# Four row blocks of a weight and two pairs of another transposed by DMA at the turn of a forward-and-backward decode kernel

## The chip, the cores and the metric

The kernel runs on one core of one Trainium2 chip. The time of a run is in device microseconds (us), for the whole kernel in one launch: a forward pass of a small transformer block for one token, and all its gradients. "PE" is the matrix engine (its weight loads are listed as PEld), "DVE" the vector engine, "ACT" the scalar engine, "SP" the engine whose queue issues nearly all DMAs of this kernel, and "POOL" the general-purpose engine. Sixteen DMA engines carry the transfers.

## The reference: what is computed

A block with one query token (x is 1 x 640), 32 heads of 192, and a key and a value cache of 8192 positions for each head. Modulation vectors (shift, scale and gate, twice) come from a second vector c. The attention half adds a gated `attention(h) @ wo`; the second half is a token mixer and an MLP of width 1536. The mixer shifts its channels by one or two tokens, so with one token it adds zeros, and x1 below is the half's input:

```python
def _A_ref(x, k_cache, v_cache, wq, wo):
    q = heads(x @ wq)                                  # 32 heads of 192
    scores = einsum('bhqd,bhkd->bhqk', q, k) * Dh ** (-0.5)
    o = einsum('bhqk,bhkd->bhqd', softmax(scores), v)
    return merged(o) @ wo                              # wo is 6144 x 640
...
h2 = _gelu(_layernorm(x1, axis=-1) @ w3) @ w4          # w3 is 640 x 1536, w4 1536 x 640
...
mod = (_silu(c) @ w_mod).reshape(c.shape[0], 6, 1, -1)
h = _layernorm(x, axis=-1) * (1 + ca) + sa
x = x + ga * _A_ref(h, A_k_cache, A_v_cache, A_wq, A_wo)
h = _layernorm(x, axis=-1) * (1 + cb) + sb
x = x + gb * _B_ref(h, B_w1, B_w2, B_w3, B_w4)
```

The outputs are x and the gradients of x, of both caches, of wq, wo, w3, w4, c and w_mod for a given gradient of x. The gradients of the caches are the largest part: as many bytes are stored as the two caches have.

## The kernel before, in words

**Forward pass.** Heads go by in a software pipeline (loop at line 652). For each head, K and V come in halves or whole (12288 bytes a partition for a half: 32 of the 64 rows that a partition holds, each of 192). DVE multiplies K by the broadcast query, PE sums the products, and the softmax weights scale K and are multiplied with V on PE. K lies in six halves of one large buffer, `k_mem`; V in four halves of `v_mem`. The two heads of a pair share one tile of Wo (`wo_t`, lines 495 to 500), with which `fwd_ao` (line 571) forms that pair's part of `o @ wo`.

**The turn.** When the last head's weights are known, the kernel must, in this order: finish o of heads 30 and 31; form the last two pairs' part of `o @ wo`; do both layer norms; form u = n2 @ W3 (60 products of a 128 x 128 block with one column, `u_mm`); the derivative of gelu and du, which also needs d_g, twelve DVE products of W4's rows with a broadcast vector (`dg_some`, line 594); dn2 = du @ W3 transposed (60 products, line 1050); the way back through the norms to dao, the gradient of the attention's output (`lnb_dao`); and do = dao @ Wo transposed for the last pair (line 1423). Only then can the gradient of V be formed and stored for the last head (line 1427 on).

**Transposed weights before.** dn2 and do take the weights transposed. PE makes them: it multiplies blocks of 128 x 128 with the identity into PSUM, four at a time (`w3T_pe`, line 759; `woT_some`, line 780), and ACT copies each group into SBUF (`w3T_act`). W3 has 60 such blocks, the last pair's Wo 15. These groups are spread by hand between the steps of the turn, through four fill points (`FILL`, lines 794 to 809) and calls in between. For the last pair but one, nothing is transposed: in the first step of the backward pass, DVE multiplies its three Wo blocks with the broadcast dao and sums along the rows (`bwd_ttr`, line 1098, called in `hook(0)`). The other pairs' do are done in batches of up to three pairs (`load_wo`, line 894; `bwd_wo_mult`).

**Loads at the turn.** `load_w` (line 637) puts W4 and W3 into freed halves of `k_mem`. All these DMAs, and the two V halves of head 29 (line 900) and the first batch of Wo (line 1021), stand on SP's queue in program order; a DMA whose buffer is still read waits there, and those behind it wait too. Each DMA also waits for the one eight places before it.

**Backward pass.** Heads go from 31 down (line 1455). For each one V is multiplied by do, summed on PE, and the gradients of V and K are formed by DVE and ACT as outer products and stored, with the other gradients' stores as jobs in between.

**Order.** Instructions of PE, DVE and ACT are pinned to the order of the program text (`pin_order`, line 53); waits between engines come from the tiles that they share. A tile counts as a whole there: the PSUM tile `sm_ps` of head 31 holds the sum of weights, o and the product with Wo side by side, and `kb_ps` holds the sums of the scaled K in its first 384 columns and, behind them (`aux_ps`), the small results of the turn.

Of the kernel before, what the change touches and what calls it, by code (L numbers as in the profile page):

```python
# [20 lines left out]
def kernel(  # L21
# [26 lines left out]
    nc = tc.nc  # L48
# [81 lines left out]
    def mul(out, a, b):  # L130
        nc.vector.tensor_tensor(out=out, in0=a, in1=b, op=ALU.mult)  # L131
# [383 lines left out]
    def fwd_tot(h, sm):  # L515
        nc.tensor.matmul(sm[:, 400:402], lhsT=ones_mat_f, rhs=rowsum[:, h - 1 : h + 1], start=True, stop=True)
# [38 lines left out]
    def fwd_o_last(h, st):  # L555
        _, _, bp, ca_, cb_ = head_split(h)
        c0 = 3 * (h // 2)
        sl = slice(bp, bp + 64)
        for o in (o_col_bf, o_col_f):
            mul(o[:, ca_ : ca_ + 1], st["o_ps"][:, 0:1], rinv_bc[:, h : h + 1])  # L560
            mul(o[sl, cb_ : cb_ + 1], st["o_ps"][sl, 1:2], rinv_bc[sl, h : h + 1])
# [171 lines left out]
    dg_some(2)  # L733
    fwd_keepB(hl - 1, st[hl - 1])
    fwd_tot(hl, sl_["sm"])
    fwd_o_mm(hl, 0, sl_)
    xp = ccol(NDC, "xp")
# [17 lines left out]
    w3T_next = [0, 0]  # L755
    w3T_ps = {}
    NG3 = NFC * NDC // 4

    def w3T_pe(n):
        for g in range(w3T_next[0], min(w3T_next[0] + n, NG3)):  # L760
            b = g % 6
            if b in (2, 4):
                w3T_ps[g] = bank("s", 2, "t_ps", SB[0])
                w3T_ps[g + 1] = w3T_ps[g][:, 512:1024]
            elif b < 2:
                w3T_ps[g] = bank("ab"[b], name="t_ps")
            for k in range(4):
                i, f = divmod(4 * g + k, NFC)
                nc.tensor.matmul(w3T_ps[g][:, k * P : (k + 1) * P], lhsT=w3n(i, f * P, (f + 1) * P), rhs=ident_bf, start=True, stop=True)
        w3T_next[0] += n  # L770

    def w3T_act(n):
        for g in range(w3T_next[1], min(w3T_next[1] + n, NG3)):
            if g % 6 in (3, 5) and g > 3:
                continue
            m = 2 if g % 6 in (2, 4) and g > 3 and g + 1 < NG3 else 1
            nc.scalar.copy(out=w3T(4 * g // NFC, 4 * g % NFC, 4 * m), in_=w3T_ps[g][:, 0 : 512 * m])
        w3T_next[1] += n

    def woT_some(n):  # L780
        for g in range(woT_next[0], min(woT_next[0] + n, 4)):
            t_ps = bank("s", 2, "t_ps", SB[0])
            blks = range(4 * g, min(4 * g + 4, 3 * NDC))
            for k, blk in enumerate(blks):
                nc.tensor.matmul(t_ps[:, k * P : (k + 1) * P], lhsT=woT[:, blk * P : (blk + 1) * P], rhs=ident_bf, start=True, stop=True)
            nc.scalar.copy(out=woT[:, 512 * g : 512 * g + P * len(blks)], in_=t_ps[:, 0 : P * len(blks)])
        woT_next[0] += n

    woT = st[HQ - 1]["wo"].rearrange("p c r -> p (c r)")
    woT_next = [0]  # L790
    fwd_ao(HH - 1, sl_["wo"], sl_["sm"], 408, False)
    ao_ps = sl_["sm"][:, 408 : 408 + NDC]
    w3T_pe(1)
    def fill0():
        w3T_act(1)
        w3T_pe(1)

    def fill1():
        w3T_act(1)
        fwd_kvK(hl - 1, 3, st[hl - 1])  # L800

    def fill2():
        pass

    def fill3():
        bwd_pf_act(HS[0])
        w3T_act(4)

    FILL = [fill0, fill1, fill2, fill3]
# [12 lines left out]
    m_ps = aux_ps[:, 64:65]  # L822

    def mean_mm(x):
        nc.tensor.matmul(m_ps, lhsT=ones_mat_f, rhs=x, start=False, stop=True, skip_group_check=True)

    mean_mm(sxp)
# [4 lines left out]
    FILL[0]()  # L832
# [3 lines left out]
    FILL[1]()  # L836
# [8 lines left out]
    w3T_t = tw.tile([P, JH, DH], BF16, name="w3T_t", tag="w3T_t").rearrange("p j d -> p (j d)")  # L845
# [3 lines left out]
    wo_src = {(PS[k], cc): st[2 * PS[k] + 1]["wo"][:, cc, :] for k in range(2) for cc in range(3)}  # L849
# [50 lines left out]
    V_b[HS[2]] = {0: load_v(bv, HS[2], 0, 4), 1: load_v(bv, HS[2], 1, 5)}  # L900
# [22 lines left out]
    w3T_pe(4)  # L923
# [5 lines left out]
    FILL[2]()  # L929
# [7 lines left out]
    FILL[3]()  # L937
# [63 lines left out]
    for i in range(NDC):  # L1001
        u_mm(i)
        if i == 2:
            w3T_pe(1)
            w3T_act(1)
        elif i == 3:
            woT_some(2)
# [3 lines left out]
    dg_some(3)  # L1011
    lnb_sums()
    w3T_pe(3)
# [5 lines left out]
    w3T_pe(5)  # L1019
    w3T_act(8)  # L1020
    load_wo(0, big_tile("V_sb"))
    lnb_map1()
    dg_some(1)
# [10 lines left out]
    def du_cols(lo, hi):  # L1034
        stt(du_bf[:, lo:hi], deriv[:, lo:hi], -1.0, d_g[:, lo:hi], ALU.mult, ALU.mult)

    f_late = dg_next[0]
    du_cols(0, f_late)
    dg_some(NFC)
    du_cols(f_late, NFC)  # L1040
# [5 lines left out]
    for i in range(NDC):  # L1046
        if i == NDC - 1:
            woT_some(1)
        for f in range(NFC):
            nc.tensor.matmul(dn2_ps[:, i : i + 1], lhsT=w3T(i, f), rhs=du_bf[:, f : f + 1], start=False, stop=(f == NFC - 1), skip_group_check=True)  # L1050
    mid_ps = {"h2": aux_ps[:, 32 : 32 + NDC]}
# [7 lines left out]
    nc.scalar.copy(out=kb_sb, in_=kb_ps[:, 0 : 2 * DH])  # L1059
# [38 lines left out]
    def bwd_ttr(hp, cc):  # L1098
        nc.vector.tensor_tensor_reduce(out=wo_src[hp, cc], in0=wo_src[hp, cc], in1=dao_bc, scale=1.0, scalar=0.0, op0=ALU.mult, op1=ALU.add, accum_out=dof[:, 3 * hp + cc : 3 * hp + cc + 1])

# [12 lines left out]

    def fin_do(lo, n):
        sl = slice(3 * lo, 3 * (lo + n))
        dve_copy(do_bf[:, sl], dof[:, sl])
# [273 lines left out]
    wo_first = [(PS[1], cc) for cc in range(3)]  # L1390
# [27 lines left out]

    do_ps = aux_ps[:, 24:27]
    for cc in range(3):  # L1420
        for j in range(NDC):
            blk = cc * NDC + j
            nc.tensor.matmul(do_ps[:, cc : cc + 1], lhsT=woT[:, blk * P : (blk + 1) * P], rhs=dao_bf[:, j : j + 1], start=False, stop=(j == NDC - 1), skip_group_check=True)
    dve_copy(do_bf[:, 3 * PS[0] : 3 * PS[0] + 3], do_ps[:, 0:3])
# [132 lines left out]
```

## Time and profile before

| | |
|---|---|
| median of 3 runs (lowest, highest) | 1362.57 us (1361.49, 1363.54) |
| the profiled execution: time, span | 1363.16 us, 1361.2 us |
| mean granted clock of PE | 0.788 |
| busy PE, PEld, DVE, ACT | 867.7, 622.0, 1083.7, 914.3 us |
| moved by DMA | 567.62 MB, mean 417 GB/s |
| HBM read, written | 339.94 MB, 225.91 MB |
| the chain of waits, by engine | DMA 41%, PE 18%, DVE 16%, ACT 5% |

The span is the time from the first to the last instruction of the profiled execution; its own time is a little longer. No engine is busy for the whole span, and the parts of the pass differ: from 20 to 500 us PE is busy for 443.41 of 480 us, from 700 to 1340 us DVE for 507.15 of 640 us. A line of the groups gives the line of the source, the engine, the operation with output and input tiles, how often it ran, the busy time, the mean length of one in ns, and the idle time ahead of it. Lines of the chain of waits give start, length and work. A window's line gives each engine's busy time, and then the granted clock, the busy share of the DMA engines and the GB/s.

### The profile page before, as it was taken

To read this page: it belongs to the slowest core of one execution; us is meant where nothing else is said; L and a number is where in the kernel's file an instruction comes from. 1 tells how busy PE (TensorE), PEld (TensorE's weight loads), DVE (VectorE), ACT (ScalarE), POOL (GpSimd) and SP (SyncE) were. 2 spreads that over 40 slices of the span, in tenths; PEclk is the share of its full clock that TensorE was granted. 3 is DMA by queue.
4 is the path that set the end of the run, shared out by engine and by line. 5 is a ranking of instruction groups with operands and counts; after the bars stand their busy time and mean duration, and the time that the engine had idled before them with its cause. 6 is when DMAs were issued, how large, how long until landed. Compare 5 with 4: busy or idle time off the path is not lost.

```text
span 1361.2 us, 27663 instructions
## 1 busy us (share of the span) xinstructions
PE 867.7 (64%) x11403; PEld 622.0 (46%) x11406; DVE 1083.7 (80%) x1247; ACT 914.3 (67%) x2558; POOL 3.2 (0%) x10
## 2 busy tenths in 40 slices
PE   4698999999999999847666754443333543242422
PEld 3577777777777777736555642111121111010100
DVE  3488888888888887899988977877668978786875
ACT  0387788778788885876767966765467745666570
POOL 0000000000000000000000000000000000000000
PEclk9799999999999999576776676676666776676766
DMA  9999999999999999799999999999999999999997
GB/s 391 417 422 428 424 416 428 425 409 427 424 417 419 422 423 401 280 396 393 426 422 427 427 431 431 430 431 430 425 433 429 432 427 428 423 434 430 433 431 335
DMA packets 46282, 567.62 MB, mean 417 GB/s; under 512 B 4685, under 2 KB 6989, under 8 KB 19405
## 3 DMA queue, kind: packets, MB, share of 16 engines
q1 hardware_dynamic: 46126, 565.86, 98.7%
q8 instruction: 89, 1.46, 0.4%
q14 instruction: 37, 0.30, 0.1%
q10 hardware_dynamic: 30, 0.00, 0.0%
HBM read 339.94 MB, written 225.91 MB: 416 GB/s over the span
## 4 chain that ended last, share of the span: by engine, by line
DMA 41%; PE 18%; DVE 16%; ACT 5%; issue 3%; DVEq 0%; SPq 0%; ACTq 0%
DMA out_dram<-k_mem 18%; DMA v_mem<-in_A_v_cache_dram 16%; DVE k_mem L1211 7%; PE dP_ps L1230 5%; PE ps_a L471 5%; ACT k_mem L1235 4%; DVE v_mem L131 3%; DMA k_mem<-in_A_k_cache_dram 3%; DMA V_sb<-in_w_mod_dram 3%; PE ps_b L482 2%; DMA out_dram<-dwo 2%; PE S_ps L411 1%; PE kb_ps L488 1%; DVE prod L131 1%; DVE V_sb L131 1%
## 5 line engine op out<-in xcount | busy, mean ns | idle before, releaser
L1235 ACT ACTIVATE k_mem<-do_pb,PF 128x192 bf16<-128x192 bf16 x1086 | 378.9, 441 | 123.7 <-DMA out_dram<-k_mem 87.7
L1230 PE MATMUL dP_ps<-v_mem,ident_bf 128*128 128x512 bf16 (+2 forms) x960 | 219.7, 403 | 264.8 <-DVE v_mem L131 264.8
L446 ACT ACTIVATE EK<-k_mem,E_f 128x192 bf16<-128x192 bf16 x992 | 355.0, 444 | 36.8 <-issue 19.4
L1230 PEld LDWEIGHTS <-ident_bf 128*128 128x128 bf16 x1056 | 120.1, 119 | 381.0 <-DVE v_mem L131 211.9
L1211 DVE TENSOR_TENSOR k_mem<-dS,q_pb 128x6144 bf16<-128x6144 bf16 x62 | 205.5, 3354 | 50.6 <-DMA out_dram<-k_mem 50.3
L131 DVE TENSOR_TENSOR v_mem<-v_mem,do_pb 128x6144 bf16<-128x6144 bf16 (+1 forms) x62 | 199.1, 3249 | 32.7 <-DMA v_mem<-in_A_v_cache_dram 32.7
L131 DVE TENSOR_TENSOR prod<-k_mem,q_pb 128x6144 bf16<-128x6144 bf16 x62 | 207.6, 3349 | 4.5 <-DMA k_mem<-in_A_k_cache_dram 3.2
L471 PE MATMUL ps_a<-EK,v_mem 128*128 128x193 bf16 x1984 | 191.5, 248 | 16.0 <-DMA v_mem<-in_A_v_cache_dram 14.8
L471 PEld LDWEIGHTS <-v_mem 128*128 128x128 bf16 x1984 | 163.7, 98 | 34.4 <-DMA v_mem<-in_A_v_cache_dram 19.7
L453 DVE TENSOR_TENSOR EK<-k_mem,P2h 128x1536 bf16<-128x1536 bf16 x124 | 117.8, 950 | 0.0
L482 PE MATMUL ps_b<-EK,v_mem 128*64 128x193 bf16 x1984 | 106.6, 249 | 0.0
L411 PE MATMUL S_ps<-prod,ident_bf 64*64 64x256 bf16 x2976 | 94.5, 273 | 6.9 <-DVE prod L131 6.9
L411 PEld LDWEIGHTS <-ident_bf 64*64 64x64 bf16 x3072 | 83.9, 109 | 26.3 <-issue 24.1
L482 PEld LDWEIGHTS <-v_mem 128*64 128x64 bf16 x1984 | 79.7, 109 | 19.1 <-issue 15.5
L1211 DVE TENSOR_TENSOR k_mem<-P2h,do_pb 128x2304 bf16<-128x2304 bf16 (+2 forms) x56 | 74.3, 1359 | 11.0 <-DMA out_dram<-k_mem 10.2
L188 ACT CAST do_pb<-bc_ps 128x384 bf16<-128x384 f32 x15 | 7.1, 472 | 96.6 <-PE bc_ps L184 96.6
L488 PE MATMUL kb_ps<-EK,hot_bf 128*32 128x384 bf16 x992 | 63.5, 333 | 0.0
L451 DVE CAST EK<-E_f 128x16 bf16<-128x16 f32 x124 | 24.4, 197 | 32.5 <-ACT EK L446 22.6
L432 ACT ACTIVATE E_f<-sm_ps,negm 128x64 f32<-128x64 f32 x31 | 9.7, 314 | 58.8 <-DVE negm L430 58.8
L415 DVE TENSOR_REDUCE S<-S_ps 128x128 f32<-128x1024 f32 x32 | 39.2, 1225 | 11.1 <-PE S_ps L411 11.0
L1339 PEld LDWEIGHTS <-ident_bf 128*128 128x128 bf16 x100 | 11.7, 117 | 75.4 <-issue 69.6
L1235 ACT ACTIVATE xt<-do_pb,PF 128x192 bf16<-128x192 bf16 x120 | 41.8, 440 | 0.1
(341 smaller groups left out, 843.2 us busy)
## 6 DMA issues: line engine op xcount, KB each, us to landing
v_mem<-in_A_v_cache_dram SPq DMA_DIRECT2D x47, 3072.0 KB, 19.5
out_dram<-k_mem SPq DMA_DIRECT2D x41, 3072.0 KB, 27.0
k_mem<-in_A_k_cache_dram SPq DMA_DIRECT2D x20, 3072.0 KB, 14.6
out_dram<-k_mem SPq DMA_DIRECT2D x33, 1536.0 KB, 19.9
v_mem<-in_A_v_cache_dram SPq DMA_DIRECT2D x25, 1536.0 KB, 16.6
k_mem<-in_A_k_cache_dram SPq DMA_DIRECT2D x24, 1536.0 KB, 18.7
out_dram<-xt SPq DMA_DIRECT2D x3, 3072.0 KB
wq<-in_A_wq_dram SPq DMA_DIRECT2D x3, 2560.0 KB, 31.2
```

The source lines that it names most:

```text
L131: nc.vector.tensor_tensor(out=out, in0=a, in1=b, op=ALU.mult)
L411: nc.tensor.matmul(st["S_ps"][c0 : c0 + 64, r, t * JH : (t + 1) * JH, :], lhsT=ident_bf[64 * r : 64 * r + 64, 64 * r : 64 * r + 64], rhs=p ...
L415: nc.vector.reduce_sum(out=st["S2"], in_=st["S_ps"], axis=AX.X)
L446: nc.scalar.activation(out=st["EK"][q][:, jj, 0:DH], in_=K_st[h, t][:, r * JQ + jj, :], func=ACT.Copy, scale=st["E_f"][:, j : j + 1])
L451: nc.vector.tensor_copy(out=EK[:, :, DH : DH + 1], in_=st["E_f"][:, q * JQ : (q + 1) * JQ, None])
L453: nc.vector.tensor_tensor(out=EK[:, NA:JQ, 0:DH].rearrange("p j (d r) -> p j d r", r=2), in0=K_st[h, t][:, r * JQ + NA : (r + 1) * JQ, :]. ...
L471: nc.tensor.matmul(st["A_ps"][:, 0:n], lhsT=V_sb[:, r * JQ + jj, a0:a1], rhs=EK[:, jj, 0:n], start=(q == 0 and jj == 0), stop=(q == 3 and ...
L482: nc.tensor.matmul(st["B_ps"][g : g + 64, 0:n], lhsT=V_sb[:, r * JQ + jj, b0:b1], rhs=EK[:, jj, 0:n], start=(q == 0 and jj < 2), stop=(q = ...
L488: nc.tensor.matmul(kb_ps[g : g + 32, 0 : 2 * DH], lhsT=hot_bf[:, HQ - 1 - h : 2 * HQ - 1 - h], rhs=EK[:, jj : jj + 2, 0:DH], start=(h == 0 ...
L1211: nc.vector.tensor_tensor(out=o.rearrange("p j (d r) -> p j d r", r=2), in0=pairs[:, :, None, :].to_broadcast([P, n, NP2, 2]), in1=vec.rea ...
L1230: nc.tensor.matmul(bst[h]["dP_ps"][:, t * JH + r : t * JH + r + n, :], lhsT=ident_bf, rhs=V_sb[:, :, k * w : (k + 1) * w], start=(k == 0), ...
L1235: nc.scalar.activation(out=o[:, jj, :], in_=vec_of(do_pb, h), func=ACT.Copy, scale=bst[h]["PF"][:, t * JH + jj : t * JH + jj + 1])
```

## The change

W4's remaining five row blocks are now loaded ahead of W3. Of W3, only row block 0 is still transposed on PE, in three groups. Row blocks 1 to 4 are read a second time from HBM by four transposing DMAs, into the buffer that before took the second half of head 29's V; that half is now loaded after the dn2 products. The Wo tiles of the last two pairs are overwritten by two transposing DMAs, and both pairs' do are formed on PE; the three DVE products and the copy in `hook(0)` are gone. The Wo product of the last pair but one moves in front of the o products of the last head, and both late Wo products are gathered in `aux_ps`. The mean of the first part of x1 is formed between the two halves of o. `fwd_o_last` writes the bf16 column first, then the Wo product follows, then the fp32 column. Three d_g products change place. The copy of `kb_sb` moves from behind dn2 to the norms.

```diff
-        elif k == 1:
-            for i in range(2):
-                nc.sync.dma_start(out=w_t[1][:, i * F : (i + 1) * F], in_=B_w3[i * P : (i + 1) * P, :])
-        else:
+        elif k == 2:
             nc.sync.dma_start(out=w_t[2][:, 0 : 5 * D]..., in_=B_w4[7 * P : 12 * P, :]...)
-            for i in range(2, 4):
+            for i in range(4):
                 nc.sync.dma_start(out=w_t[1][:, i * F : (i + 1) * F], in_=B_w3[i * P : (i + 1) * P, :])
...
-    fwd_keepB(hl - 1, st[hl - 1])
     fwd_tot(hl, sl_["sm"])
+    ao_ps = aux_ps[:, 65 : 65 + NDC]
+    fwd_ao(HH - 2, st[hl - 2]["wo"], aux_ps, 65, False)
+    fwd_rinv(hl, sl_["sm"])
+    fwd_keepB(hl - 1, st[hl - 1])
     fwd_o_mm(hl, 0, sl_)
+    fwd_o_prev(hl - 1)
...
-    fwd_rinv(hl, sl_["sm"])
-    fwd_o_prev(hl - 1)
+    mean_mm(sxp)
     dg_some(3)
     fwd_o_mm(hl, 1, sl_)
-    fwd_o_last(hl, sl_)
-    fwd_ao(HH - 2, st[hl - 2]["wo"], sl_["sm"], 408, False)
+    fwd_o_last(hl, sl_, o_col_bf)
+    fwd_ao(HH - 1, sl_["wo"], aux_ps, 65, False)
+    fwd_o_last(hl, sl_, o_col_f)
...
+    def w3T_pe(g):
+        ps = bank("ab"[g % 2], name="t_ps")
+        for k in range(4):
+            f = 4 * g + k
+            nc.tensor.matmul(ps[:, k * P : (k + 1) * P], lhsT=w3n(0, f * P, (f + 1) * P), rhs=ident_bf, start=True, stop=True)
+        nc.scalar.copy(out=w3T(0, 4 * g, 4), in_=ps)
+
+    woT = {k: st[2 * (HH - 1 - k) + 1]["wo"].rearrange("p c r -> p (c r)") for k in range(2)}
...
-    FILL[0]()
+    dg_some(1)
+    w3T_pe(0)
...
-    FILL[1]()
+    dg_some(1)
+    fwd_kvK(hl - 1, 3, st[hl - 1])
+    w3T_pe(1)
...
-    V_b[HS[2]] = {0: load_v(bv, HS[2], 0, 4), 1: load_v(bv, HS[2], 1, 5)}
+    w3T_t = flat(v_tile(bv, 5))
+    for i in range(1, NDC):
+        nc.sync.dma_start(out=w3T(i, 0, NFC).rearrange("p (f r) -> p f r", r=P), in_=B_w3[i * P : (i + 1) * P, :], transpose=True)
+    for k in range(2):
+        nc.sync.dma_start(out=woT[k].rearrange("p (j r) -> p j r", r=3 * P), in_=A_wo[3 * PS[k] * P : 3 * (PS[k] + 1) * P, :], transpose=True)
+    V_b[HS[2]] = {0: load_v(bv, HS[2], 0, 4)}
...
-    w3T_pe(4)
...
-    FILL[2]()
+    nc.scalar.copy(out=kb_sb, in_=kb_ps[:, 0 : 2 * DH])
...
-    FILL[3]()
+    w3T_pe(2)
+    bwd_pf_act(HS[0])
...
-        woT_some(1)
...
         u_mm(i)
-        if i == 2:
-            w3T_pe(1)
-            w3T_act(1)
-        elif i == 3:
-            woT_some(2)
...
-    dg_some(3)
     lnb_sums()
-    w3T_pe(3)
+    dg_some(NFC)
...
-    w3T_pe(5)
-    w3T_act(8)
     load_wo(0, big_tile("V_sb"))
-    lnb_map1()
-    dg_some(1)
...
-    f_late = dg_next[0]
-    du_cols(0, f_late)
-    dg_some(NFC)
-    du_cols(f_late, NFC)
+    stt(du_bf, deriv, -1.0, d_g, ALU.mult, ALU.mult)
+    lnb_map1()
     lnb_map2()
...
+    V_b[HS[2]][1] = load_v(bv, HS[2], 1, 5)
...
-    nc.scalar.copy(out=kb_sb, in_=kb_ps[:, 0 : 2 * DH])
...
         if i == 0:
-            for u in wo_first:
-                bwd_ttr(*u)
-            fin_do(PS[1], 1)
             bwd_dob(PS[1])
...
+    do_mm(0)
+    do_out(0)
     do_pb[PS[0]] = pair_bc2(bsm, do_bf, PS[0], "do_pb")
-    o0 = tw.tile([P, JH, DH], BF16, name="dV", tag="w3T_t")
+    o0 = tw.tile([P, JH, DH], BF16, name="dV")
     bwd_dv_dve(o0, HS[0], 0, 0, (8, 16, JH))
+    do_mm(1)
     h2_mm()
+    do_out(1)
```

`do_mm(k)` is the loop of 15 products of line 1423 for one of the two pairs, with the blocks in the order in which the transposing DMA lays them; `do_out(k)` is the copy behind it.

More of the change, by code (lines that the diff above doesn't have):

```diff
@@ L553, in fwd_o_prev, with fwd_o_last @@
         dve_copy(o_col_bf[bp : bp + 64, cb_ : cb_ + 1], o_col_f[bp : bp + 64, cb_ : cb_ + 1])
-    def fwd_o_last(h, st):
+    def fwd_o_last(h, st, o):
         _, _, bp, ca_, cb_ = head_split(h)
@@ L558, in fwd_o_last @@
         sl = slice(bp, bp + 64)
-        for o in (o_col_bf, o_col_f):
-            mul(o[:, ca_ : ca_ + 1], st["o_ps"][:, 0:1], rinv_bc[:, h : h + 1])
-            mul(o[sl, cb_ : cb_ + 1], st["o_ps"][sl, 1:2], rinv_bc[sl, h : h + 1])
+        mul(o[:, ca_ : ca_ + 1], st["o_ps"][:, 0:1], rinv_bc[:, h : h + 1])
+        mul(o[sl, cb_ : cb_ + 1], st["o_ps"][sl, 1:2], rinv_bc[sl, h : h + 1])
     def fwd_o_rows(hp, sm):
@@ L740, with mean_mm @@
     nc.vector.tensor_tensor_reduce(out=T5[:, 0, :], in0=xp, in1=ZW[:, 0, :], scale=-1.0 / D, scalar=0.0, op0=ALU.mult, op1=ALU.add, accum_out=sxp)
-    fwd_rinv(hl, sl_["sm"])
-    fwd_o_prev(hl - 1)
+    m_ps = aux_ps[:, 64:65]
+    def mean_mm(x):
+        nc.tensor.matmul(m_ps, lhsT=ones_mat_f, rhs=x, start=False, stop=True, skip_group_check=True)
+    mean_mm(sxp)
     dg_some(3)
     fwd_o_mm(hl, 1, sl_)
-    fwd_o_last(hl, sl_)
-    fwd_ao(HH - 2, st[hl - 2]["wo"], sl_["sm"], 408, False)
+    fwd_o_last(hl, sl_, o_col_bf)
+    fwd_ao(HH - 1, sl_["wo"], aux_ps, 65, False)
+    fwd_o_last(hl, sl_, o_col_f)
     SB = [1024]
@@ L753, in w3T @@
         return w_t[2][:, 5 * D + f * P : 5 * D + (f + n) * P]
[L755 to L787, printed above, removed]
@@ L844 @@
     tw = tw_cm.__enter__()
-    w3T_t = tw.tile([P, JH, DH], BF16, name="w3T_t", tag="w3T_t").rearrange("p j d -> p (j d)")
     HS = list(range(HQ - 1, -1, -1))
@@ L848 @@
     V_b = {HS[0]: st[HS[0]]["V"], HS[1]: dict(enumerate(st[HS[1]]["V"]))}
-    wo_src = {(PS[k], cc): st[2 * PS[k] + 1]["wo"][:, cc, :] for k in range(2) for cc in range(3)}
     wo_b = {}
@@ L1112, in bwd_wo_red @@
         nc.vector.reduce_sum(out=dof[:, 3 * lo : 3 * (lo + n)], in_=ps, axis=AX.X)
-    def fin_do(lo, n):
-        sl = slice(3 * lo, 3 * (lo + n))
-        dve_copy(do_bf[:, sl], dof[:, sl])
     def fin_do_rows(lo, n):
@@ L1388 @@
     J2[NPH + 14].append(job_c)
-    wo_first = [(PS[1], cc) for cc in range(3)]
     fins = {min(2 + 2 * b, NPH - 1): b for b in range(len(BATCHES))}
@@ L1417, in hook, with do_mm, do_out @@
             dq[i] = (PS[1], 2, fin_dq_mm(PS[1], 2))
[L1419 to L1424, printed above, removed]
+    do_ps = aux_ps[:, 24:30]
+    def do_mm(k):
+        for cc in range(3):
+            for j in range(NDC):
+                lo = (3 * j + cc) * P
+                nc.tensor.matmul(do_ps[:, 3 * k + cc : 3 * k + cc + 1], lhsT=woT[k][:, lo : lo + P], rhs=dao_bf[:, j : j + 1], start=False, stop=(j == NDC - 1), skip_group_check=True)
+    def do_out(k):
+        dve_copy(do_bf[:, 3 * PS[k] : 3 * PS[k] + 3], do_ps[:, 3 * k : 3 * k + 3])
+    do_mm(0)
+    do_out(0)
     do_pb[PS[0]] = pair_bc2(bsm, do_bf, PS[0], "do_pb")
-    o0 = tw.tile([P, JH, DH], BF16, name="dV", tag="w3T_t")
+    o0 = tw.tile([P, JH, DH], BF16, name="dV")
     bwd_dv_dve(o0, HS[0], 0, 0, (8, 16, JH))
+    do_mm(1)
     h2_mm()
+    do_out(1)
     bwd_dv_dve(big_half(big_order.pop(0)), HS[0], 1, 0, (JQ, JH))
```

29 lines of the change are left out of this document (1 added, 28 removed).

## The prediction

> **What bounds the kernel now.** I read the page first: the 40 slices and the table of queues. The DMA engines carry the kernel's queue for 98.7% of the span, and of the slices of 34 us only the seventeenth falls below 9 tenths, with 280 GB/s.
>
> ```profile
> span 1361.2 us, 27663 instructions
> DMA  9999999999999999799999999999999999999997
> GB/s 391 417 422 428 424 416 428 425 409 427 424 417 419 422 423 401 280 396 393 426 422 427 427 431 431 430 431 430 425 433 429 432 427 428 423 434 430 433 431 335
> q1 hardware_dynamic: 46126, 565.86, 98.7%
> ```
>
> That slice covers 544 to 578 us: the turn, where the forward pass ends and the first gradients can be stored. The windows over it give, after the engines' busy times, the granted clock, the DMA share and the GB/s in the last three columns:
>
> ```profile
> 546.00:548.00 2.00, 2.00 (x35) 2.00 (x34) 1.64 (x8) 1.51 (x5) 0.00 (x0) 0.50 0.99 416
> 548.00:553.00 5.00, 5.00 (x82) 5.00 (x80) 4.22 (x19) 4.24 (x8) 0.00 (x0) 0.50 0.53 221
> 553.00:558.00 5.00, 4.41 (x83) 4.05 (x80) 3.71 (x21) 3.59 (x7) 0.00 (x0) 0.50 0.83 291
> 558.00:562.00 4.00, 3.05 (x84) 3.07 (x85) 2.10 (x6) 2.51 (x9) 0.00 (x0) 0.50 0.07 27
> 562.00:574.00 12.00, 7.19 (x77) 7.00 (x75) 11.90 (x14) 12.00 (x36) 2.09 (x2) 0.50 0.96 384
> 574.00:578.00 4.00, 4.00 (x56) 4.00 (x55) 3.11 (x4) 3.86 (x12) 0.00 (x0) 0.75 0.51 140
> ```
>
> Idle DMA, by the share: 2.35 + 0.85 + 3.72 + 0.48 + 1.96 = 9.4 us. By bytes lost against 420 GB/s: 2.4 + 1.5 + 3.7 + 1.0 + 2.7 = 11.3 us. Everywhere else from 20 to 1340 us the share is 1.00 or more. So the time is DMA work plus some 10.4 us of holes. The change can win no more than those holes, and every DMA microsecond that it adds counts in full once they are closed.
>
> Last I read the chain of waits and the groups from 540 to 562 us, for what makes the holes:
>
> ```profile
> 551.00 3.41 PE t_ps L769 x32
> 554.41 1.31 PE kb_ps L1050 x48
> ...
> L769 PE MATMUL t_ps<-ident_bf,k_mem 128*128 128x128 bf16 x60 | 7.3, 311 | 0.0
> ...
> L785 PE MATMUL t_ps<-ident_bf,wo_t 128*128 128x128 bf16 x15 | 2.1, 305 | 0.0
> ```
>
> PE's transposes of W3 (L769) and Wo (L785) stand in the chain at the half clock, ahead of dn2 (L1050); the first store waits behind them.
>
> **The change, part by part.** *Computing in the turn.* 48 of 60 W3 transposes leave PE (48/60 of 7.3 = 5.8 us) and all 15 of Wo (2.1), with their ACT copies; added are 15 small matmuls for the second pair's do (0.5 us, as L1423 takes for 15). Not all of this is on the chain. Going along it:
> - The Wo product moved in front of o, now in its own PSUM tile, no longer waits for the second pair of o writes: PE stood 1.14 us there until 541.73. PE gets 0.5 us more before o; about 0.5 us is won. Two d_g products put into the chain on DVE (0.75 us each, partly beside PE) take it back. n2 near 547.2 as before: 0.
> - The 60 u products, without 4 + 8 transposes between them, end near 549.2 instead of 550.5. DVE still has three d_g products there until 549.9, so u is won by 0.65 us.
> - du: before, PE's 32 transposes end at 554.42 and one d_g product stands in DVE's way. After, 1.9 us of small DVE steps from 549.9 give 551.8; dn2 starts 2.4 us sooner. Without 4 transposes inside, T comes at 554.1, not 556.5.
> - do: 1.7 us of steps as before, without PE's wait for the kb_sb copy (0.4), which moves to where ACT waits for DVE. First dV at 557.7, not 560.4: 2.7 us sooner, if the transposed blocks have landed.
> - In the first hook three products of 0.82 us (L1099) go, 2.5 us of DVE at 579.6, beside saturated DMA: 0.
>
> *The six transposing DMAs.* W3's blocks 1 to 4 are 1.57 MB, two pairs' Wo 0.98 MB: 2.56 MB that come a second time, on SP's queue ahead of everything else of the turn. The built instructions name source tiles of 16 rows by 128 columns, so rows of 256 bytes, 9984 of them. No transposing DMA is in this trace, so the price is bounded by its packets. Two windows of the DMA view, 586 to 590 us (nearly all 12288-byte packets) and 512.5 to 513.5 us (113 packets of 1280 bytes, 20 large ones):
>
> ```profile
> DMA packets 156, 1.72 MB, mean 430 GB/s; under 512 B 16, under 2 KB 16, under 8 KB 16
> q1 hardware_dynamic: 156, 1.72, 101.3%
> ```
> ```profile
> DMA packets 144, 0.39 MB, mean 390 GB/s; under 512 B 11, under 2 KB 124, under 8 KB 124
> q1 hardware_dynamic: 144, 0.39, 99.4%
> ```
>
> The first: 1.013 x 16 x 4 us over 140 packets is 463 ns for 12288 bytes. The second: 15.9 us less 20 x 463 ns leaves 59 ns for 1280 bytes. The line through both is 12 ns a packet plus 36.7 ns per 1000 bytes, so 21 ns for 256 bytes. 9984 x 21 / 16 engines = 13.1 us (195 GB/s). Ends: at the copy rate, 430 GB/s, 5.9 us; if every 32 bytes written to a partition (16 rows of 2 bytes) paid the bare 12 ns, 60 us. I take 13.1, since the reads are known and the rows nearest to them; how writes are gathered no row shows.
>
> The Trainium skill ("DMA: Bandwidth & Descriptors", Latency and other measured facts) gives 261 GB/s for a DMA transpose whose middle dimension is not contiguous, and 350 to 400 for a contiguous one; here rows of 256 bytes lie 3072 or 1280 bytes apart, the first kind. By it the six would cost an estimated 9.8 us in place of 13.1. The Trainium skill's "Advanced Engine Details and Errata" (X-Bar Transpose (TRN2)) calls them as fast as regular DMAs, an estimated 6.4 to 7.3 us. No run shown here decides between these.
>
> *Landing.* The V halves issued at 538.5 and 539.8 landed 11.9 and 15.6 us later (550.4, 555.4); half the engines lag, as the 0.53 share shows. Less 3.9 us for the first half, W3's last block is there at 546.5. At 195 GB/s its transposed blocks land by 554.6 and the first Wo by 557.1: the last dn2 products wait about 1 us, do 1.2 us, and the first dV comes at 558.9, still 1.5 us early. The second Wo lands at 559.6, before DVE asks for it.
>
> *SP's queue.* The V half that goes behind dn2 (issued near 554, not 539.8), load_wo (no longer held until 552.85 by L769's reads) and the first V half land 11 us of copies behind the transposes; they are used in the second and third heads after 590 us, and the DMAs in flight cover the issue. dV's stores stand behind the moved half, which then waits only for work that they need too. W4's rest ahead of W3 makes W3 wait some 3 us longer for the last reads of head 30's K; a Wo load issued at 525.91 took 13.8 us to land, so that backlog hides it: 0. It would cost what is left uncovered if those reads came past 535 us.
>
> *Sum.* The queue now holds transposes, V, Wo and V from 546 until near 570, and the first stores are ready by 559 to 560: the holes close, but for an assumed 0.5 us. 13.1 - 10.4 + 0.5 = +3.2 us. The profiled execution took 1363.16 us, 0.6 above the median of the runs; on the median, 1362.57 + 3.2 = 1365.8. Its own range, by holes of 9.4 to 11.3 us and 11.5 to 16 us of price: 1363 to 1370.
>
> **The rivals.**
> - *Copy rate (other side).* Six transposes at 5.9 us: 5.9 - 10.4 + 0.5 = -4.0, 1358.6. For it: the transposes move the same bytes as the plain loads of these weights, which ran at 397 GB/s from 530 to 546 us among V halves. Against: 256-byte rows, and the window of 1280-byte packets already falls to 390 GB/s. It decides below 9.9 us (258 GB/s), where added work equals the closed holes.
> - *A draw.* Between 7.5 and 11.5 us the two cancel: near 1362.6. The Trainium skill's 261 GB/s would be this one.
> - *Far slower.* If the written pieces or SP's time for issuing (a plain DMA: 0.33 us; there is cover for some 8 us of it) set the rate, 20 us and more: dn2 and do then wait for their blocks and the price shows in full, e.g. 25 - 10.4 = +15, 1377.
> - *The holes stay.* If the backward pass cannot fill them because its buffers free late, the hole of 574 to 578 us (2.0 to 2.7 us) remains on top: 1368. Against: that hole follows stores that come after waits on DVE and PE, and these are earlier now.
>
> **How the numbers follow.** The sum's case 0.45 (0.32 of it over 0.2% slower; the holes that stay are 0.07 of it), copy rate 0.25 (0.24 faster), a draw 0.17 (0.12 same, 0.05 faster), far slower 0.13. Within 0.2%, 2.7 us, is about what the runs can't tell from no change, as their own spread is 0.15%. Faster 0.29, same 0.26, slower 0.45. The range takes in copy rate at the low end and most of the far slower at the high one: 1358.5 to 1378.
>
> **What would show it.** Right: DMA share near 1.0 from 546 to 580, six transposes together some 13 us of it, first dV near 559, no t_ps group but 12 products. Wrong: bytes per us near 400 while the transposes run (copy rate), or dn2 waiting for V_sb past 556 us with DMA share low (issue or written pieces).

## The result and the profile after

The changed kernel takes 1366.97 us (median of 6 runs, 1366.32 to 1368.09); the kernel before took 1362.10 us on the same chip (6 runs, 1361.49 to 1363.54). The ratio is 1.0036, 95% interval 1.0025 to 1.0046: 4.9 us slower, where 3.2 us were forecast. In the experiments below every kernel is compared with runs of the kernel before on its own chip, whose median lay between 1361.75 and 1362.57 us.

The page of the changed kernel:

```profile
span 1366.1 us, 27553 instructions
DMA  9999999999999999999999999999999999999997
GB/s 392 417 425 425 421 421 424 420 422 420 421 416 421 424 422 366 326 394 423 425 425 426 427 426 434 428 431 425 429 425 432 429 425 429 429 432 429 433 430 327
DMA packets 56457, 570.17 MB, mean 417 GB/s; under 512 B 14860, under 2 KB 17164, under 8 KB 29580
q1 hardware_dynamic: 56302, 568.42, 99.7%
```

The dip to 7 tenths in the seventeenth slice is gone: the DMA engines are busy there. But they move little: 366 and 326 GB/s in the two slices from 512 to 581 us. The kernel moves 570.17 MB instead of 567.62, and 14,860 packets of under 512 bytes instead of 4685: the transposed weights.

The windows over the turn (the same ones as before; the granted clock, the DMA share and the GB/s stand last; the share adds up the times of the packets, so it exceeds 1 where these overlap):

```profile
546.00:548.00 2.00, 0.88 (x8) 0.72 (x7) 0.37 (x2) 1.35 (x4) 0.00 (x0) 0.50 1.04 217
548.00:553.00 5.00, 2.21 (x62) 2.11 (x62) 4.43 (x21) 1.43 (x5) 0.00 (x0) 0.50 1.19 189
553.00:558.00 5.00, 2.51 (x62) 2.23 (x61) 3.53 (x23) 0.00 (x0) 0.00 (x0) 0.50 1.16 164
558.00:562.00 4.00, 3.13 (x94) 2.79 (x95) 2.43 (x4) 2.15 (x7) 0.00 (x0) 0.50 1.14 350
562.00:574.00 12.00, 8.29 (x90) 7.89 (x88) 11.90 (x14) 8.10 (x24) 1.28 (x2) 0.51 1.00 396
574.00:578.00 4.00, 0.43 (x8) 0.26 (x5) 1.10 (x1) 0.68 (x2) 0.00 (x0) 0.89 1.01 423
```

PE is relieved (2.21 us busy from 548 to 553, where it was full), and the holes of 558 to 562 and 574 to 578 us are closed. In their place the rate is 164 to 217 GB/s from 546 to 558. It is low earlier too: 540 to 546 us ran at 400 GB/s in the kernel before (the first line) and runs at 255 now (the second).

```profile
540.00:546.00 6.00, 4.68 (x75) 3.72 (x73) 3.25 (x19) 1.67 (x4) 0.00 (x0) 0.50 1.04 400
```
```profile
540.00:546.00 6.00, 3.92 (x61) 2.81 (x59) 3.65 (x20) 0.58 (x1) 0.00 (x0) 0.50 1.28 255
```

The loss can be counted in bytes, against 420 GB/s. Before, 540 to 578 us lost 0.3 + 11.3 = 11.6 us. After, the windows lose 2.4 (540 to 546) + 1.0 + 2.75 + 3.05 + 0.7 + 0.7 + 0 = 10.5 us, and the 2.55 MB more take 6.1 us at 420 GB/s. 10.5 + 6.1 - 11.6 = +5.0 us; the two spans differ by 4.9.

From 543.6 us on the chain of waits goes through SP, which issues the transposing DMAs, and the first Wo's landing, where PE's transposes stood in the kernel before (start, length, what):

```profile
544.32 3.23 SPq L855
547.60 1.75 SPq L855
549.40 1.92 SPq L855
...
551.43 6.55 DMA wo_t<-in_A_wo_dram
...
559.74 3.50 DVE dV L1144 x3
563.26 13.88 DMA out_dram<-dV
```

The timeline shows who waits for the blocks (start, length, then the instruction; in brackets the idle time ahead of it and what ended it):

```profile
555.55 0.48 PE L990 MATMUL kb_ps<-du_bf,V_sb 128*128 128x1 bf16 x12 [0.54 <-DMA V_sb<-in_B_w_dram]
558.03 0.56 PE L1354 MATMUL kb_ps<-dao_bf,wo_t 128*128 128x1 bf16 x15 [1.11 <-DMA wo_t<-in_A_wo_dram]
559.74 3.50 DVE L1144 TENSOR_TENSOR dV<-P2h,do_pb 128x1536 bf16<-128x1536 bf16 x3 [0.95 <-ACT do_pb L393]
```

The last 12 of dn2's products wait 0.54 us for W3's last block, the do products 1.11 us for the first Wo; the first dV comes at 559.74 us, 0.64 us earlier than before:

```profile
560.38 1.83 DVE L1211 TENSOR_TENSOR dV<-P2h,do_pb 128x1536 bf16<-128x1536 bf16 x2 [0.95 <-ACT do_pb L393]
```

### The profile page after: what moved, and what is told of

It reads as the page before. It is cut to its first block, busy times and chain, and to the rows that moved or that the text cites. A ratio compares the mean times of both kernels' runs of the same rounds, so it can differ in the third digit from the quotient of the medians.

```text
span 1366.1 us, 27553 instructions
## 1 busy us (share of the span) xinstructions
PE 874.3 (64%) x11358; PEld 621.7 (46%) x11358; DVE 1080.9 (79%) x1240; ACT 905.4 (66%) x2545; POOL 2.4 (0%) x10
## 2 busy tenths in 40 slices
DMA packets 56457, 570.17 MB, mean 417 GB/s; under 512 B 14860, under 2 KB 17164, under 8 KB 29580
## 4 chain that ended last, share of the span: by engine, by line
DMA 52%; PE 21%; DVE 15%; ACT 6%; issue 3%; SPq 3%; DVEq 0%; ACTq 0%
DMA out_dram<-k_mem 23%; DMA v_mem<-in_A_v_cache_dram 22%; DVE k_mem L1144 7%; PE ps_a L471 7%; ACT k_mem L1168 5%; PE ps_b L482 4%; DMA k_mem<-in_A_k_cache_dram 3%; DMA V_sb<-in_w_mod_dram 3%; PE dP_ps L1163 3%; DVE v_mem L131 3%; PE S_ps L411 2%; PE kb_ps L488 2%; SPq L234 1%; DVE prod L131 1%; DMA out_dram<-dV 1%
## 5 line engine op out<-in xcount | busy, mean ns | idle before, releaser
L1163 PE MATMUL dP_ps<-v_mem,ident_bf 128*128 128x512 bf16 (+2 forms) x960 | 223.6, 410 | 251.6 <-DVE v_mem L131 251.6
L1163 PEld LDWEIGHTS <-ident_bf 128*128 128x128 bf16 x1056 | 122.6, 122 | 369.7 <-DVE v_mem L131 207.6
L1272 PEld LDWEIGHTS <-ident_bf 128*128 128x128 bf16 x100 | 12.3, 123 | 79.7 <-issue 75.5
```

The costliest lines, as they stand in the source:

```text
L1163: nc.tensor.matmul(bst[h]["dP_ps"][:, t * JH + r : t * JH + r + n, :], lhsT=ident_bf, rhs=V_sb[:, :, k * w : (k + 1) * w], start=(k == 0), ...
```

## The experiments

**Is it the transposing at all?** Three kernels replace or remove the six transposing DMAs. None of them transposes these weights, so dn2, do and the gradients behind them are not the reference's; only the time is read.

The first copies the same bytes without transposing, in the long rows in which the weights lie:

```
-  dma_start(out=w3T(i, 0, NFC).rearrange("p (f r) -> p f r", r=P), in_=B_w3[i*P:(i+1)*P, :], transpose=True)
+  dma_start(out=w3T(i, 0, NFC), in_=B_w3[i*P:(i+1)*P, :])
-  dma_start(out=woT[k].rearrange("p (j r) -> p j r", r=3*P), in_=A_wo[3*PS[k]*P:3*(PS[k]+1)*P, :], transpose=True)
+  dma_start(out=woT[k].rearrange("p (c r) -> p c r", r=D), in_=wo_v[:, 3*PS[k]:3*PS[k]+3, :])
```

> The changed kernel with its six transposing DMAs as plain DMAs of the same 2.56 MB into the same tiles (long runs, nothing transposed: dn2 and both do's use untransposed weights, so the gradients behind them are left out of account). Theory (the transposing DMAs are slow: 18.9 us from first packet to last landing, where a copy of as many bytes takes about 6): the six take 6 to 7 us, the first dV comes near 558 to 559 us, and the time falls by 6 to 9 us, to 1358 to 1361. Rival (the doubled bytes, the moved V half and the new order of the turn cost the time, whatever way the bytes are laid): 1365 to 1367.

Measured: 1359.37 us, ratio 0.9979 (0.9970 to 0.9988). The windows of this kernel:

```profile
548.00:553.00 5.00, 2.21 (x62) 2.10 (x62) 4.43 (x21) 1.43 (x5) 0.00 (x0) 0.50 1.05 380
553.00:558.00 5.00, 2.90 (x77) 2.63 (x76) 3.57 (x24) 0.00 (x0) 0.00 (x0) 0.50 0.99 387
```

The engines do nearly the same work as in the changed kernel; what differs is the last column, 380 and 387 GB/s instead of 189 and 164. So all of the loss hangs on how these six DMAs run.

The second copies them plainly too, but in pieces of 256 bytes (four DMAs for W3, six for Wo):

```
+  half = w3T_t[:, ...].rearrange("p (f two r) -> p f two r", two=2, r=P)
+  dma_start(out=half[:, :, (i-1) % 2, :], in_=B_w3[i*P:(i+1)*P, :].rearrange("p (f r) -> p f r", r=P))
+  for cc in range(3):
+      dma_start(out=woT[k].rearrange("p (j c r) -> p c j r", c=3, r=P)[:, cc], in_=wo_v[:, 3*PS[k]+cc, :].rearrange("p (j r) -> p j r", r=P))
```

> As the run with plain copies, but every run of 256 bytes is a piece of its own (the four blocks of W3 interleaved two by two, Wo in three DMAs a pair; still nothing transposed, the weights' use is left out of account as there). Theory (the price is that of 256-byte pieces, 18 to 21 ns each): the six cost 11 to 13 us and the time stays at 1364 to 1367. Rival (transposing itself, through the issue on SP's queue of 1.7 to 5.4 us a DMA or through engines that wait for one another, is the price): the pieces take 6 to 9 us and the time is 1359 to 1362.

Measured: 1365.96 us, ratio 1.0027 (1.0017 to 1.0036), with 224 and 211 GB/s from 548 to 558 us:

```profile
548.00:553.00 5.00, 2.21 (x62) 2.10 (x62) 4.46 (x20) 1.77 (x6) 0.00 (x0) 0.50 1.01 224
553.00:558.00 5.00, 2.70 (x76) 2.53 (x76) 3.78 (x25) 0.00 (x0) 0.00 (x0) 0.50 0.95 211
```

Small pieces alone bring 3.8 of the 4.9 us back. What transposing adds is 1.1 us against the changed kernel's six DMAs, but these are ten DMAs: a kernel below with ten transposing DMAs is 7.2 us over the kernel before, 3.4 us more than these. Nor does this run part the pieces from their issue, for SP was held 0.64 to 4.09 us by each of the ten, and only 0.33 to 0.81 us by each of the six plain copies in long rows.

The third has none of the six DMAs:

```
-  (the six DMAs)
-  w3T_t = flat(v_tile(bv, 5))
+  V_b[HS[2]] = {0: load_v(bv, HS[2], 0, 4), 1: load_v(bv, HS[2], 1, 5)}
+  w3T_t = flat(V_b[HS[2]][1])
```

> The changed kernel without the six DMAs: the V half is loaded in its old place, and dn2 takes that V half for W3's blocks, do the untransposed Wo (the gradients behind them are left out of account). It shows what the rest of the change is worth. Theory (the holes close only as far as the first store comes sooner, by some 2 us): 1359 to 1361. Rival (the new order of the turn is itself slower, since the step from the norms' sums to n2 ended at 548.7 in place of 547.0): 1362 or more.

Measured: 1359.51 us, ratio 0.9981 (0.9972 to 0.9990). The holes are there again:

```profile
553.00:558.00 5.00, 3.04 (x77) 2.70 (x76) 3.45 (x23) 0.00 (x0) 0.00 (x0) 0.50 0.68 275
558.00:562.00 4.00, 3.37 (x87) 3.09 (x86) 3.01 (x4) 3.16 (x10) 0.00 (x0) 0.50 0.27 101
```

The plain copies in long rows fill these holes for nothing (1359.37 against 1359.51 us). The transposing ones cost 4.9 + 2.6 = 7.5 us over none, each taken against its own kernel before.

**Does the late n2 matter?** The forecast had n2 unchanged. In the changed kernel `n_bf`, its operand for u, comes at 548.72 us instead of 547.02: a copy of transposed W3 stands in ACT's queue ahead of the square root and waits for PE.

```profile
546.55 0.58 ACT L765 CAST k_mem<-t_ps 128x512 bf16<-128x512 f32 x1 [2.25 <-PE t_ps L764]
547.03 0.30 ACT L148 ACTIVATE lnp<-lnp,eps_c 128x1 f32<-128x1 f32 x1
```

The edit moves that group behind the norms:

```
     fwd_kvK(hl - 1, 3, st[hl - 1])
-    w3T_pe(1)
...
+    w3T_pe(1)
     w3T_pe(2)
```

> The changed kernel, with the second group of W3's PE transposes moved behind the norms' small steps, so that its ACT copy no longer stands ahead of the square roots. Theory (the chain of computing is covered by DMA work): n2 comes 1.5 us sooner, dn2 then waits that much longer for W3's transposed blocks, and the time stays within 0.5 us of 1367. Rival (the late n2 is what made the change slower than the sum said): 1365.5.

Measured: 1366.95 us, ratio 1.0037 (1.0024 to 1.0049). `n_bf` comes at 546.94 us and dn2 starts at 551.81, 1.8 us sooner; then dn2 waits 1.33 us for the last block, and the do products for theirs:

```profile
555.26 0.48 PE L990 MATMUL kb_ps<-du_bf,V_sb 128*128 128x1 bf16 x12 [1.33 <-DMA V_sb<-in_B_w_dram]
559.33 3.49 DVE L1144 TENSOR_TENSOR dV<-P2h,do_pb 128x1536 bf16<-128x1536 bf16 x3 [0.95 <-ACT do_pb L393]
```

1.8 us won early are 0.4 us at the first dV and nothing in the time. The DMA, not the computing, sets this stage.

**Price by the rows, or by the DMA?** Three kernels change the number of rows and of DMAs. The first takes W3's four transposes as one DMA over the same rows:

```
-  for i in range(1, NDC):
-      dma_start(out=w3T(i, 0, NFC)..., in_=B_w3[i*P:(i+1)*P, :], transpose=True)
+  dma_start(out=w3T_t.rearrange("p (f r) -> p f r", r=4*P), in_=B_w3[P:5*P, :], transpose=True)
```

> The four transposing DMAs of W3's blocks become one DMA over the same 6144 rows of 256 bytes; Wo's two stay, so SP issues three transposing DMAs in place of six. Theory (the price is that of 256-byte pieces, 21 ns each on 16 engines, whatever the number of DMAs): 1366 to 1368 us, as the changed kernel. Rival (SP, which is held 1.7 to 5.4 us per transposing DMA, or a fixed price per DMA sets the pace): at least 2 us less, 1362 to 1365 us.

Measured: 1365.29 us, ratio 1.0021 (1.0012 to 1.0030); its kernel before took 1362.21. It is 3.1 us over the kernel before, the changed kernel 4.9: 1.8 us less, just outside the theory's range and short of the rival's 2 us. The intervals of the two ratios overlap a little, but the traces are plain. Here is the transfer rate of the changed kernel from 540 to 564 us, in 40 slices of 0.6 us:

```profile
GB/s 390 374 356 261 205 205 205 202 179 171 104 232 292 145 191 280 178 237 273 145 31 288 296 8 9 191 290 238 133 108 288 502 147 348 328 430 410 410 320 420
```

And of the kernel with one DMA for W3:

```profile
GB/s 366 356 288 256 245 219 217 174 189 160 164 290 291 290 291 290 291 290 327 47 121 61 286 290 209 201 289 464 246 389 410 471 410 361 360 422 416 424 397 474
```

From the twelfth slice (546.6 us) the single DMA keeps 290 GB/s over seven slices, falls to 47 to 121 GB/s ahead of Wo's first, rises to 290 again, falls to 201 between the two Wo, and is done. The changed kernel reaches the same 280 to 296 GB/s, but falls between any two of its six DMAs. The packets in the two traces show what happens there. Most rows of 256 bytes take 18 ns each; but of the 9538 that the changed kernel reads from 546.3 us on, 63 take 0.4 to 1.3 us, in four groups, and those of a group end together, at 548.6, 552.6, 555.1 and 557.8 us. The kernel with one DMA for W3 has one such group, of 11 rows, and in the kernel with plain pieces of 256 bytes no piece takes more than 0.07 us. So at the seams between transposing DMAs packets stand until all go on together; why they do, no run here shows. So 290 GB/s, 14 ns for 256 bytes on 16 engines, is what the rows cost; the rest of the 21 ns that I had put on each row belongs to the DMAs. The last Wo landed 2.6 us sooner than in the changed kernel (557.2 against 559.8 us; a landing here is the median of the DMA's 16 completion events in the trace). The theory as I had put it on record, a price per piece alone, falls.

The second leaves only W3's blocks 3 and 4 (without Wo's two and blocks 1 and 2), the third only W3's four:

```
-  for i in range(1, NDC):   (W3)
+  for i in range(3, NDC):   (W3; the second kernel alone)
-  for k in range(2): ...    (Wo; both)
```

> Of the six transposing DMAs only those of W3's blocks 3 and 4 stay (3072 rows of 256 bytes in place of 9984); blocks 1 and 2 are read from the places of 4 and 3, and Wo's two pairs are multiplied untransposed, so the outputs behind them are wrong. Theory (13.0 us for 9984 rows and some 2 us of waiting for the slower half of the engines, about 7.5 us of it hidden in time in which the DMA engines idle anyway, since six of them cost 7.4 us over none): 4.0 + 2 us fit into the hidden part, 1359 to 1360.5 us, as with none. Rival (the wait for the slower half at the start, or the first transposing DMA itself, is a fixed price that nothing hides): at least 2 us over none, 1361.5 us or more. Rival (price in proportion to the rows, nothing hidden): 0.31 of 7.4 us over none, 1361.8 us.

> The four transposing DMAs of W3 stay (6144 rows), Wo's two are left out; Wo's two pairs are multiplied untransposed, so the outputs behind them are wrong. Theory (a hidden part of 7.5 us, then 1.3 us per 1000 rows): 8.0 + 2 - 7.5 = 2.5 us over none, 1361.3 to 1363 us. Rival (in proportion to the rows): 0.62 of 7.4 us over none, 1364.1 us. Rival (only Wo's late landings cost, since the chain waits for them; W3's come in time): 1359 to 1360.5 us.

Measured: 1358.53 us, ratio 0.9968 (0.9956 to 0.9981), with two blocks; 1361.38 us, ratio 0.9994 (0.9985 to 1.0003), with four. Two blocks cost nothing over none, four cost 1.8 us, all six DMAs 7.5, each taken against its own kernel before. Two even ended 0.5 us below their theory's range and 1.0 us below none, which nothing here explains; four lie inside theirs, and the rival that only Wo's late landings cost falls. A price in proportion to the rows (1361.8 and 1364.1 us) falls, and so does a fixed price that nothing hides: the idle DMA time that the change leaves in the turn takes up the first 3072 rows, and what goes beyond it counts.

To separate the number of DMAs from the longer written runs of the one large DMA, one more kernel cuts each W3 transpose in two:

```
+  for f in (0, 6):
+      dma_start(out=w3T(i, f, 6)..., in_=B_w3[i*P:(i+1)*P, f*P:(f+6)*P], transpose=True)
```

> The changed kernel with each of W3's four transposing DMAs cut into two of 768 rows (ten transposing DMAs in all, the same 9984 rows of 256 bytes from the same addresses). In the transfer rates by 0.6 us, the transposing DMAs of the changed kernel run at 285 to 290 GB/s with a dip of 60 to 160 GB/s between one and the next, and the 6144 rows as one DMA keep 290 GB/s over nine slices. Theory (a row costs 14 ns on 16 engines, 8.8 us for the 9984, and each DMA some 0.7 us besides, (13.0 - 8.8) / 6): four more DMAs cost 2.8 us, 1368.7 to 1371 us. Rival (the one DMA over all four blocks was quicker for its longer runs, 1024 bytes on the side it writes, and the number of DMAs costs nothing): 1366 to 1367.7 us.

Measured: 1368.95 us, ratio 1.0049 (1.0035 to 1.0063), its kernel before at 1361.75: 7.2 us over it, 2.3 more than the changed kernel, for the same rows. Its rates over the same 24 us:

```profile
GB/s 386 402 353 279 207 205 200 205 207 172 122 58 264 81 234 276 245 135 134 154 38 193 218 18 10 192 272 126 90 273 289 183 84 239 291 342 307 471 328 348
```

More dips, and the last Wo lands at 561.8 us, 2.0 us later than in the changed kernel. Three DMAs fewer won 1.8 us, four more cost 2.3: about 0.6 us a DMA, near the (13.0 - 8.8) / 6 = 0.7 us of the rates. Either step alone is small, and its two intervals overlap a little; from three DMAs to ten (ratios 1.0012 to 1.0030 and 1.0035 to 1.0063) they do not. The rival, that the number costs nothing, falls.

**What happens from 542 to 546 us?** In the changed kernel the rate falls to 205 GB/s and below from 542.4 us on, four microseconds before the rows flow, and in the kernels above with other transposing DMAs the windows from 542 to 546 us hold 177 to 236 GB/s; the plain pieces of 256 bytes hold 270 and 258, the plain copies in long rows run on at 344 to 373. The completion events of W3's fourth natural block (issued at 536.04 us) come at 540.3 to 541.3 us from one half of the DMA engines and at 543.8 to 545.9 from the other: one half runs at least 2.5 us ahead, 4.4 us by the medians. I took it that this half stands idle until the other has caught up, since nothing but transposes is queued.

The packets bear this out. Of the 9984 rows, 272 are read from 540.9 to 543 us, none from 543 to 544, and 42 from then until 546. Twelve of the first 272 begin between 541.4 and 542.4 us and all end at 546.7, after 4.4 to 5.3 us, and in the kernels with plain copies no piece takes over 1.3 us there. In those the quicker half's completion events of W3's last natural block come at 541.2 to 542.9 us; in the changed kernel 14 of the 16 events come together, at 546.8 to 546.9. It is not PE that holds the start: the view of waits puts 5.1 us of SP's first hold down to PE (L764), but rows were already being read at 540.9 us, and the plain DMA in the same place was issued in 0.33 us at 538.52.

The next run tries whether V's first half, put on another queue, fills that time:

```
-  V_b[HS[2]] = {0: load_v(bv, HS[2], 0, 4)}              (behind the transposes, SP's queue)
+  V_b[HS[2]] = {0: load_v(bv, HS[2], 0, 4, nc.scalar)}   (ahead of them, ACT's queue)
```

> The changed kernel, with V's first half issued from ACT's queue ahead of the transposing DMAs and not behind them on SP's; so that ACT is free for it, the three copies of W3's block 0 stand behind the norms. Theory (from 542 to 546 us the faster half of the DMA engines only waits, since SP's ring has nothing but transposes ahead; V's half of 0.98 MB fills that time): 542 to 546 us go from 190 to 214 GB/s to 300 or more, and the time falls by some 2 us to 1364 to 1365.5 us. Rival (the engines' time is taken all the same, or the transposes only start later): 1366.3 us or more.

Measured: 1367.69 us, ratio 1.0039 (1.0027 to 1.0052). The rate was 392 and 293 GB/s in the two windows, but nothing was won. It was no clean test: PE stood idle until 546.7 us for W3's first block, which the V half had delayed, and SP held its first transposing DMA for 7.7 us until V's half had landed, as the scheduler gave both the same semaphore. A second try put PE's groups directly ahead of u and V's load behind the first transposing DMA in the order written:

```
     for i in range(1, NDC):
         (transposing DMA of block i)
+        if i == 1:
+            V_b[HS[2]] = {0: load_v(bv, HS[2], 0, 4, nc.scalar)}
```

> Again V's first half from ACT's queue, but issued behind the first transposing DMA in the order written, so that no transposing DMA waits for the semaphore of V's half (as SP did for 7.7 us in the run before); and PE's three groups of W3's block 0 stand directly ahead of u, so that PE does not wait there for block 0's landing. Theory (the faster half of the DMA engines can take V's half from 542 to 546 us while the transposes wait for the slower half, some 2 us won): 542 to 546 us at 300 GB/s or more, and 1364 to 1365.7 us. Rival (V's half only delays W3's last blocks and with them the start of the transposes, so nothing is won): 1366.3 us or more, with the rate of 542 to 546 us high all the same.

Measured: 1367.28 us, ratio 1.0036 (1.0023 to 1.0048). The order that was built again had V's load first, and SP waited again (engine, line, releaser, us, times, longest), as the waits show:

```profile
SPq L858 <- DMA k_mem<-in_A_v_cache_dram: 7.8, 1, 7.8
```

Its rates from 540 to 564 us:

```profile
GB/s 412 413 389 410 428 381 363 379 260 189 200 210 189 244 277 201 125 250 290 134 207 134 54 293 1 9 208 276 200 266 193 92 185 290 275 130 223 289 246 218
```

V's half does fill 540 to 544.8 us at 363 to 428 GB/s. Then a fall to 189 to 260 GB/s follows, from 544.8 to 548 us: the two halves of the engines are no closer together after it, W3's last block now landing by 545.9 us on one half and at 550.4 on the other. So the fall was moved, not filled, as the rival said; but SP issued its first transposing DMA only at 546.68 us, so from 545.9 us until then the quicker half had nothing queued, and this run does not tell whether V's half could have filled the wait. That the transposes stand is shown by the packets of the changed kernel. That it costs about 2 us (2.4 us by bytes from 540 to 546, 0.3 in the kernel before, 1.7 with the plain pieces) follows from the rates; no run here took it away, so the price is argued and not shown.

**A version of both.** By the runs above some 3000 to 5000 rows in few DMAs are free. So W3's blocks 3 and 4 come by one transposing DMA, blocks 0 to 2 go through PE in nine groups, and the pair before the last is done on DVE as in the kernel before. In one version the last pair's Wo goes through PE, in the other it comes by a second DMA:

```
+  dma_start(out=w3T_t[:, 0:2*F].rearrange("p (f r) -> p f r", r=2*P), in_=B_w3[3*P:5*P, :], transpose=True)
+  dma_start(out=woT[0]..., in_=A_wo[3*PS[0]*P:3*(PS[0]+1)*P, :], transpose=True)   (the second version alone)
+  w3T_pe(1, 2, 3)   (ahead of the norms; their ACT copies behind n2)
+  w3T_pe(4, 5)      (behind u)
+  w3T_pe(6, 7, 8)   (behind the sums of lnb_sums)
```

> A version of both kernels: W3's blocks 3 and 4 come transposed by one DMA (3072 rows of 256 bytes), blocks 0 to 2 are transposed on PE in nine groups, the last pair's Wo on PE and the pair before on DVE, as in the kernel before; V's half stays behind dn2, o and Wo as in the changed kernel. Theory (3072 rows are hidden, and the PE groups fit into PE's idle time ahead of u and ahead of dn2): 1358.5 to 1360.5 us, 1.5 to 3.5 us under the kernel before. Rival (six PE groups and their ACT copies, or Wo's work behind dn2, hold the first dV back as before): 1361.5 to 1363 us, no gain.

> As the mixed version with blocks 3 and 4 by one DMA, but the last pair's Wo comes transposed by a second DMA (4992 rows in all) and the pair before is done on DVE. Theory (7.5 us hidden, 1.3 us per 1000 rows, 2 us of waiting at the start: 6.5 + 2 - 7.5 = 1.0 us over none): 1359.5 to 1361.5 us, behind the other mixed version by 0 to 1 us. Rival (Wo on PE and its copies on ACT are what holds the first dV): 0.5 us or more ahead of the other mixed version.

Measured: 1360.97 us, ratio 0.9986 (0.9977 to 0.9995), with Wo on PE; 1359.97 us, ratio 0.9983 (0.9974 to 0.9992), with Wo by DMA. Both beat the kernel before, by 1.6 and 2.6 us, and the changed one by far. The first ended 0.5 us above its theory's range and below the rival's. The two can't be told apart by their intervals, but the second's order is as its rival had it: its first dV came at 557.12 us, the first's at 558.58.

```profile
552.10 1.45 PE L1007 MATMUL kb_ps<-du_bf,V_sb 128*128 128x1 bf16 x48
555.43 0.54 PE L1381 MATMUL kb_ps<-dao_bf,wo_t 128*128 128x1 bf16 x15 [0.91 <-DVE dao_bf L134]
557.12 3.50 DVE L1168 TENSOR_TENSOR dV<-P2h,do_pb 128x1536 bf16<-128x1536 bf16 x3 [0.95 <-ACT do_pb L393]
```

These are the timeline's lines of the second version: the last 48 of dn2's 60 products run through without a wait, and do waits for DVE, not for Wo. With two transposing DMAs the blocks come in time.

## Why the prediction was right, and where not

The direction, the cause and most of the size were right: 1365.8 us was forecast on the median, 1366.97 came; the rival of the other side (copy rate, 1358.6) is what the plain copies give, 1359.4. Step by step:

- *Holes of 10.4 us that the change closes.* Right in kind: the share is 1.00 or more from 558 us on. By bytes the holes were 11.3 us, the upper of the two values.
- *The price of the six, 13.1 us.* All but 446 of the 9984 rows flowed from 546.3 to 559.3 us, 13.0 us. The sum was right, its parts were not: a 256-byte row costs 14 ns and not 21 (290 GB/s while one DMA runs, so 8.8 us for 9984 rows), and about 0.7 us more goes to each of the six DMAs, much of it in packets that stand at the seams. The line through packets of 1280 and 12288 bytes put too much on the small packet, and there was no term for a DMA. That the two errors cancelled is luck: the same 13.1 us would have been 2.3 us too low with ten DMAs and 1.8 too high with three. The Trainium skill ("DMA: Bandwidth & Descriptors", Latency and other measured facts) states 261 GB/s for such a transpose: within one DMA the traces show 290, over the six 197 (2.56 MB in 13.0 us). The draw did not come.
- *Start of the transposes.* The forecast let them start when W3 had landed (546.5 us; it landed at 546.9) and let the DMA engines work at full rate until then. That is the step that failed: 540 to 546 us lost 2.1 us more than before, while the first transposing packets stood until 546.7 us for the slower half of the engines. The term of the sum that was missing is this one; the errors of the others nearly cancel (13.0 for 13.1 us of price, 1.2 for 0.5 of rest, holes of 11.3 for 10.4).
- *What is left of the holes, 0.5 us.* By bytes 1.2 us (from the end of the transposes at 559.3 us to 574 us, at 386 GB/s). With the values that were measured the sum is 13.0 + 2.1 + 1.2 - 11.3 = +5.0 us, against 4.9 of the runs.
- *n2 near 547.2, as before.* Wrong by 1.7 us (548.72 for 547.02): ACT's copy stood ahead of the square root. It cost nothing, as the run with the copy moved shows.
- *u, du and dn2.* dn2 started 0.6 us sooner, not 2.4, because of that copy; the last block landed at 555.5 us (554.6 forecast), the first Wo at 557.9 (557.1), the second at 559.8 (559.6). The first dV came at 559.74 us, not 558.9.
- *SP's queue covered.* SP was held for 1.7 to 5.4 us per transposing DMA, where the six plain copies in long rows took 0.33 to 0.81, and so appears in the chain. V's halves landed later, and nobody waited for them.
- *The rival of holes that stay* falls: 574 to 578 us ran at 423 GB/s. *Far slower* falls too.

## What to carry to other kernels

A DMA-bound kernel can take over work from a compute engine for nothing as long as the DMA time that this adds fits into idle DMA time of the same stage: count the added time at the rate of the pieces that it really moves (here 290 GB/s for 256-byte rows, against 420), plus a price for each DMA (here 0.6 us), and move only as much as fits. Here two blocks in one DMA and one Wo fitted and, with the other blocks left on PE, won 2.6 us, while all six DMAs lost 4.9. A price got by a line through packets five times larger may come out right in total and still be wrong in its parts, which shows as soon as the DMAs are merged or cut.

## What was not expected of the hardware

- Transposing DMAs on one queue do not run into each other: in the changed kernel the rate falls from some 290 to between 8 and 180 GB/s between one and the next, and packets of 256 bytes, most of 18 ns, stand there for up to 1.3 us and end together. The same rows cost 1.8 us less in three DMAs and 2.3 us more in ten than in six. Plain DMAs of 256-byte pieces showed the same ceiling (291 GB/s in their best slices of 0.6 us) and 3.8 of the 4.9 us of loss, but no such standing packet (none over 0.07 us).
- At the start of the first transposing DMA the rate fell to about half for 4 us (177 to 236 GB/s), while one half of the DMA engines finished its plain copies 4.4 us after the other; the transposing packets begun until then stood up to 5.3 us, until 546.7. Plain copies in long rows in the same place ran on at 344 to 373 GB/s (542 to 546 us).
- Issuing a transposing DMA of 0.39 to 0.49 MB held SP for 1.7 to 5.4 us, the one of 1.57 MB for 11.7 us; the six plain copies in long rows held it for 0.33 to 0.81 us, but the ten in pieces of 256 bytes (0.16 to 0.39 MB) for 0.64 to 4.09. So transposing alone is not what holds it.
